# A gated mix of attention and GLU: earlier loads for the token mixtures, dense products thinned out over fourteen periods, and one early sigmoid in pieces

## The chip, the core and the metric

The program runs on one core of a Trainium2 chip. The metric is the device time of one execution in microseconds (us). The engines in the text are TensorE (PE in the profile, its weight loads PEld), VectorE (DVE), ScalarE (ACT), GpSimd (POOL) and SyncE (SP, which here issues all DMAs).

## What is computed

With x of 2048 tokens and 512 features:

```python
def _A_ref(x, wqkv, wo):                      # 32 heads of 16
    q, k, v = ...                             # x @ wqkv, by heads
    p = softmax(q @ k.T * Dh ** -0.5)
    return (p @ v) @ wo
def _B_ref(x, w_gate, w_up, w_down):          # F = 1792
    return (sigmoid(x @ w_gate) * (x @ w_up)) @ w_down
g = sigmoid((x * gate_w).sum(-1))
out = g * _A_ref(x) + (1 - g) * _B_ref(x)
```

All is float32 in and out. A dense product is made from three faster products of split operands: each operand is a high part (`h`, a rounded copy) and a low part (`l`, what the copy left over), and high x high, high x low and low x high are summed in PSUM.

## The kernel before, in words

**The main loop** (line 733 on) has 256 periods, `k`. A period belongs to one pair of heads and handles two key tiles. Its parts are generators, and a string of words says in which order TensorE calls them: `m0` and `m1` (line 695) make a score tile for head 0 or 1 of the pair 20 steps ahead and have VectorE take its row maximum (line 268); `t0` and `t1` (`st_part`, line 547) make scores the other way round with the maximum already taken off, and ScalarE writes their exponential (line 560); `d1` and `d0` (`dense`) put one matmul of the running dense product (`Sum.half`, line 150) on the upper or lower half of the array, so that it runs beside a score matmul on the other half. `values(k)` (line 666) closes the period with 16 matmuls of probabilities by values (line 674) into bank `seven[0]`, which the profile calls sm0. The digits in the words name PSUM banks: 0 to 3 are sm0 to sm3, 4 to 6 are st0 to st2, 7 is dn. The running dense product sums in dn.

The order is STEADY (eight m, eight t, six d1, six d0) for the first 239 periods, BARE (the same m and t, no dense product, dn used as an eighth score bank) for seven, and LAST (eight t, three d1, three d0; the maxima are all taken) for the last ten. From there on VectorE, not ScalarE, copies finished products and value sums out of PSUM.

**Tokens.** Both halves of the array write into dn. Between the upper and the lower half of a product stands a token: an empty GpSimd instruction (`turn`, line 161) that waits for the last upper matmul and on which the first lower one waits. GpSimd works in order, so a token also waits for what stands ahead of it there.

**Queues.** GpSimd's steps wait in lists: `later` (value sums, weight splits, the last maxima's row), `slow` (token mixtures, taken when `later` is empty) and `soon` (sums of finished products, moved to `later` at the period's end). `work(length)` puts out steps from these lists until their listed costs use up the length: after each turn and at the end of each period. `flush` puts out a whole list.

**Dense products.** A job list (`filling`, line 342) runs beside the attention: the remaining query and key columns, then the gate and up products by a scheme with fewer multiplications: `far`, `side` and `chain` products. `side` and `chain` need differences of token tiles, the mixtures, which `mix_x` (line 303) loads (line 308) and hands to GpSimd as differences and splits; four of them go out after the first four `far` jobs. Mixtures, key and query splits, old results (`had`) and late weights share two buffers, tag "ev"; product results and mixture halves share four, tag "er".

**The end** (line 824 on) takes 28 chunks (`n`) of 24 matmuls: hidden = sigmoid(gate) x up from memory (`hidden`, line 628), split in high and low (`hidden_split`, line 643), times the down weights (line 850), and between them eight groups of 24 matmuls for the attention's output (`heads_out`). Hidden values are loaded four chunks ahead. For chunks 0 and 1 `hidden_early` (line 634) makes the sigmoid inside the last periods from an exponential, since ScalarE's table holds the exponential there: 1/(1 + exp(-x)) with one VectorE reciprocal of 128x1024 each. `denominators` (line 647) loads the sums of the softmax, inverts them and stores them for `heads_load`: for one half of the heads in period 251, for the other at chunk 9.

Of the kernel before, what the change touches and what calls it, by code (L numbers as in the profile page):

```python
# [24 lines left out]
P = 128  # L25
# [13 lines left out]
FULL = 239  # L39
# [6 lines left out]
def gated_mix(ctx, tc, x, xT, wqk, wv, wo, w_gate, w_up, w_down, gate_w, out):  # L46
# [255 lines left out]

    def mix_x(c, k):


        one, two = [keep.tile([P, 2, 512], F32, name=f"mix{i}_{c}{k}", tag="ev", bufs=2) for i in range(2)]
        for to, (ci, ki) in ((one[:, 0], (c + 2, k)), (one[:, 1], (c, k)), (two[:, 0], (c + 2, k + 2)), (two[:, 1], (c, k + 2))):
            sp.dma_start(to, xT[ci, ki])

        def minus(to, u, w):  # L310
            slow.append((1.3, lambda: pool.tensor_tensor(to, u, w, ALU.subtract)))
        minus(one[:, 1], one[:, 0], one[:, 1])
        cols = slice((c + 2) * 512, (c + 3) * 512)
        split_later(xh[:, k, cols], xl[:, k, cols], one[:, 1], queue=slow)
        minus(one[:, 0], two[:, 0], one[:, 0])
        minus(two[:, 0], two[:, 0], one[:, 1])
        minus(two[:, 1], two[:, 1], two[:, 0])
        for n, t in enumerate((two[:, 0], one[:, 0], two[:, 1])):
            put_mix(n, c, k, t)
# [21 lines left out]
    def filling():  # L341
# [132 lines left out]
        for job, nxt in zip(jobs, jobs[1:]):  # L474
            due = len(later)
            kind, n = job
            coming = None
            for at, run in enumerate(sums_of(kind, n, ws)):
                if at == ask[kind][0]:
                    coming = raws(*nxt)  # L480
                if at == ask[kind][1]:
                    new = weights(*nxt, coming)
                    end = later[-1]
                yield run
            while end in later:
                later.pop(0)[1]()
            ws = new
            if kind == "far" and n < 4:
                flush(slow)
                mix_x(n // 2, n % 2)  # L490
            if kind == "far" and n == HF - 1:
                flush(slow)
                for c in range(2):
                    mixed_x(0, c, 2, c)
# [98 lines left out]
    eight = seven + [dn]  # L593
# [40 lines left out]
    def hidden_early(m):  # L634

        gu = loaded[m]
        act.activation(gu[:, 0], gu[:, 0], AF.Exp, scale=-1.0)
        dve.tensor_scalar(gu[:, 0], gu[:, 0], 1.0, 3e38, op0=ALU.add, op1=ALU.min)
        dve.reciprocal(gu[:, 0], gu[:, 0])  # L639
        dve.tensor_tensor(gu[:, 1], gu[:, 0], gu[:, 1], ALU.mult)  # L640

# [5 lines left out]
    def denominators(i):  # L647
        rows = slice(64 * i, 64 * i + 64)
        sp.dma_start(den[rows, :], pv_d[i].rearrange("p (c r) q -> (p c) r q", r=32)[:, DH, :])
        dve.reciprocal(den[rows, :], den[rows, :])  # L650
# [60 lines left out]
    def emit(order, **parts):  # L711

        for word in order.split():
            if word == "turn":
                turn(run)
                work(1.3)
            else:
                kind, _, b = word.partition(":")
                spot[:] = [eight[int(b)]] if b else []
# [5 lines left out]
    BARE = ("m1:7 t0:5 m1:2 t0:1 m1:3 t0:6 m1:0 t0:4 "  # L725
            "m0:7 t1:5 m0:2 t1:1 m0:0 t1:6 m0:3 t1:4")
# [6 lines left out]
    for k in range(NPER):  # L733
# [13 lines left out]
        emit(STEADY if k < FULL else BARE if k < FREE else LAST, **parts)  # L747
# [15 lines left out]
        if n == NSTEP - 10:  # L763
            denominators(0)
        if k == NPER - 2:
            raws = [late_raw(*late[m][:2]) for m in range(2)]
        if k in (NPER - 6, NPER - 4):
            hidden_early((k - NPER + 6) // 2)

    flush(later)  # L770
    bank = turns(banks)
    hidden_split(0, dve)
    act.activation(g1, logit, AF.Sigmoid)
    dve.tensor_scalar(g0, g1, -1.0, 1.0, op0=ALU.mult, op1=ALU.add)
# [3 lines left out]
    hidden(2)  # L778
# [33 lines left out]
    bankt = turns(maxb + [dn])  # L812
    bankh = turns(banks)
# [26 lines left out]
    for n, (c, f) in enumerate(chunks):  # L840
# [5 lines left out]
        for t in range(4):  # L846
# [4 lines left out]
            if (n, t) == (0, 1):  # L851
                values(NPER - 1)
                flush(later)
                hidden_split(1, dve)
# [4 lines left out]
        if n == 9:  # L859
            denominators(1)  # L860
# [36 lines left out]
```

## Time and profile before

| what | value |
|---|---|
| median of three runs | 1784.79 us (1781.0 to 1790.31) |
| the profiled execution | 1784.94 us |
| its span, first to last instruction | 1783.2 us, so 1.7 us lie around it |
| granted TensorE clock, mean | 0.977 |
| busy: PE, DVE, ACT, POOL | 1721.3, 1434.0, 1357.2, 873.2 us |

Rows of a group or of the timeline have start and length in us, engine, line, operation, "out<-in" with buffer numbers left out, shapes, a count, and in brackets the idle time just before and what ended it. Matmul ends are modelled and overlap. In windows each engine's entry is busy time and number of instructions; then come the granted clock, the share of the DMA engines and GB/s.

### The profile page before, as it was taken

What the parts mean: (1) busy time and instruction counts of PE and PEld (TensorE: products, weight loads), DVE (VectorE), ACT (ScalarE), POOL (GpSimd) and SP (SyncE); (2) the same over time, 40 slices, a digit from 0 to 9 for tenths busy, and PEclk for the clock granted to TensorE, in tenths of its full rate; (3) what the DMA queues carried; (4) which work ended last, traced back from release to release, by engine and by line L of the source; (5) the groups of instructions that cost most, each with busy time, mean ns of one, the idle gap of its engine ahead of it and who ended that gap; (6) DMA issues with size and microseconds to landing.
All of it is one profiled execution on the core that took longest, in us unless ns stands there. A gap on an engine that the chain in (4) does not pass through costs nothing.

```text
span 1783.2 us, 34285 instructions
## 1 busy us (share of the span) xinstructions
PE 1721.3 (97%) x12450; PEld 1040.4 (58%) x12450; DVE 1434.0 (80%) x2295; ACT 1357.2 (76%) x2631; POOL 873.2 (49%) x849
## 2 busy tenths in 40 slices
PE   9999999998899999999999999999999988698999
PEld 7755555554455555555555555555555543276787
DVE  6988888876789999998888888888888884653654
ACT  4288888877788888888888888888888886642321
POOL 1043434347635555555566666666666652352110
PEclk9999999999899999999999999999999997899999
DMA  9312414154645353536353535353434330186762
GB/s 250 76 50 58 94 58 94 58 123 169 181 132 143 98 123 106 110 107 159 134 125 112 125 114 125 114 126 115 124 115 126 115 126 8 52 259 217 234 200 76
DMA packets 124617, 219.83 MB, mean 123 GB/s; under 512 B 23008, under 2 KB 32992, under 8 KB 121568
## 3 DMA queue, kind: packets, MB, share of 16 engines
q1 hardware_dynamic: 124448, 217.64, 42.7%
q8 instruction: 98, 1.61, 0.4%
q14 instruction: 71, 0.58, 0.1%
HBM read 129.24 MB, written 88.34 MB: 122 GB/s over the span
## 4 chain that ended last, share of the span: by engine, by line
PE 88%; DVE 3%; DMA 3%; ACT 1%; issue 1%; POOL 1%; SPq 1%; POOLq 0%; DVEq 0%; ACTq 0%
PE dn L150 27%; PE sm L674 26%; PE sm L266 12%; PE st L558 6%; PE sm L850 4%; PE sm L558 4%; PE st L266 2%; PE st L137 2%; DVE stat L268 2%; PE st L150 1%; PE dn L850 1%; DMA gul<-gu_d 1%; PE st L524 1%; ACT p L560 1%; DVE gul L639 1%
## 5 line engine op out<-in xcount | busy, mean ns | idle before, releaser
L268 DVE TENSOR_REDUCE stat<-sm 128x1 f32<-128x512 f32 x1317 | 850.4, 681 | 176.4 <-PE sm L558 137.6
L560 ACT ACTIVATE p<-st 128x512 f32<-128x512 f32 x1034 | 620.7, 645 | 4.0 <-PE st L558 3.7
L560 ACT ACTIVATE p<-sm 128x512 f32<-128x512 f32 x1012 | 598.9, 627 | 31.3 <-PE st L558 17.4
L266 PE MATMUL sm<-ks,qs 48*128 48x512 f32 x1317 | 524.8, 439 | 5.3 <-DVE stat L268 4.8
L674 PE MATMUL sm<-p,v 128*17 128x512 f32 x4032 | 494.2, 608 | 6.8 <-DVE stat L268 6.8
L268 DVE TENSOR_REDUCE stat<-st 128x1 f32<-128x512 f32 x717 | 467.7, 680 | 0.2 <-PE st L266 0.2
L558 PE MATMUL st<-qs,ks 64*128 64x512 f32 x1034 | 436.3, 425 | 0.0
L558 PE MATMUL sm<-qs,ks 64*128 64x512 f32 x1012 | 426.7, 424 | 0.6 <-ACT p L560 0.6
L266 PEld LDWEIGHTS sm<-ks,qs 48*128 48x128 f32 x1317 | 240.5, 185 | 298.9 <-DVE stat L268 215.9
L691 POOL TENSOR_TENSOR sum<-sum,part 128x512 f32<-128x512 f32 x224 | 289.1, 1291 | 246.9 <-PE sm L558 213.0
L266 PE MATMUL st<-ks,qs 48*128 48x512 f32 x717 | 283.1, 395 | 0.0
L679 ACT ACTIVATE part<-sm 128x512 f32<-128x512 f32 x215 | 128.9, 599 | 153.1 <-issue 114.2
L674 PEld LDWEIGHTS sm<-p,v 128*17 128x17 f32 x4032 | 94.5, 98 | 242.6 <-issue 163.4
L558 PEld LDWEIGHTS st<-qs,ks 64*128 64x128 f32 x1034 | 192.4, 187 | 30.9 <-issue 5.7
L558 PEld LDWEIGHTS sm<-qs,ks 64*128 64x128 f32 x1012 | 188.2, 187 | 11.4 <-issue 4.3
L466 POOL TENSOR_TENSOR had<-chain,had 128x512 f32<-128x512 f32 x84 | 108.0, 1285 | 64.3 <-PE sm L558 36.1
L266 PEld LDWEIGHTS st<-ks,qs 48*128 48x128 f32 x717 | 133.8, 187 | 1.4 <-ACT v L541 0.3
L466 POOL TENSOR_TENSOR chain<-chain,chain 128x512 f32<-128x512 f32 x84 | 108.6, 1293 | 23.0 <-PE st L558 11.7
L100 POOL TENSOR_TENSOR ol<-ot,oh 128x1024 fp32r<-128x1024 f32 x8 | 19.3, 2413 | 122.3 <-ACT oh L97 110.8
L466 POOL TENSOR_TENSOR side<-side,side 128x512 f32<-128x512 f32 x28 | 36.2, 1291 | 79.6 <-PE sm L558 74.2
L497 ACT ACTIVATE chain<-dn 128x512 f32<-128x512 f32 x107 | 73.7, 689 | 0.0
L850 PE MATMUL sm<-wd_h,hl 128*128 128x512 f32 x208 | 67.4, 391 | 0.0
(752 smaller groups left out, 3149.0 us busy)
## 6 DMA issues: line engine op xcount, KB each, us to landing
gul<-gu_d SPq DMA_DIRECT2D x56, 512.0 KB
had<-gu_d SPq DMA_DIRECT2D x84, 256.0 KB
gu_d<-had SPq DMA_DIRECT2D x84, 256.0 KB
gu_d<-side SPq DMA_DIRECT2D x56, 256.0 KB
qs<-q_d SPq DMA_DIRECT2D x90, 128.0 KB
ks<-k_d SPq DMA_DIRECT2D x90, 128.0 KB
pv_d<-sum SPq DMA_DIRECT2D x32, 256.0 KB
gu_d<-far SPq DMA_DIRECT2D x28, 256.0 KB
```

What stands on the lines that cost most here:

```text
L137: pe.matmul(o, a, b, start=(i == 0), stop=(i == len(ops) - 1))
L150: mm = pe.matmul(self.o, a[rows], b[rows], start=(self.n == 0), stop=(self.n == 2 * len(self.ops) - 1))
L266: pe.matmul(t, qs[r:r + KM, qt * P:(qt + 1) * P], ks[r:r + KM, g * 512:(g + 1) * 512], start=True, stop=True)
L268: dve.tensor_reduce(stat[half][:, b, qt % 8, g:g + 1], t, axis=AX.X, op=ALU.max)
L466: pool.tensor_tensor(to, u, w, ALU.add)
L497: leave = lambda e, o: act.activation(e, o, AF.Copy)
L558: pe.matmul(o, ks[r:r + KR, (kt + a) * P:(kt + a + 1) * P], qs[r:r + KR, q0:q0 + 512], start=True, stop=True)
L560: act.activation(pt[:, 2 * a + c, :], o, AF.Exp, scale=DH ** -0.5)
L674: pe.matmul(o[32 * c:32 * c + VW, :], v[:, 2 * k % 16 + a, h * VW:(h + 1) * VW], pts[c // 2][:, 2 * a + c % 2, :], start=(a == 0), stop=(a ...
L679: act.activation(e, o, AF.Copy)
L691: pool.tensor_tensor(s, s, e, ALU.add)
L850: pe.matmul(down[t], a, b, start=(f == 0 and m == 0), stop=(f == NF - 2 and m == 5))
```

## The change

Five edits are made together.

1. `mix_load` is split from `mix_x`: the loads of mixture u go out at product 6u + 2 of the `far` jobs, its GpSimd steps at product 6u + 4. Before, both stood after job u.
2. After each turn `work` is given 2.0, not 1.3.
3. STEADY ends at period 232; periods 232 to 245 use HALF, which is STEADY with three d1 and three d0 left out and the same banks; BARE is gone.
4. Only chunk 0 has its sigmoid from the exponential. It begins in period 249, the reciprocal is four pieces of 128x256, one a period, and the split into hl0 follows in period 254. Chunk 1 takes ScalarE's sigmoid after the loop and its split on ScalarE; chunk 2's sigmoid comes after chunk 0's matmuls.
5. `denominators` becomes a generator of load, two reciprocals of 64x256, and store: the first half loads in period 250 and is inverted at chunks 0 and 1, the second loads at chunk 1, is inverted at chunks 5 and 6, and is stored at chunk 7. The banks of the end's products are dealt out anew.

```diff
-FULL = 239
+FULL = 232
...
+    def mix_load(c, k):
+        tiles = mixing[c, k] = [keep.tile([P, 2, 512], F32, name=f"mix{i}_{c}{k}", tag="ev", bufs=2) for i in range(2)]
+        for t, ki in zip(tiles, (k, k + 2)):
+            for a, ci in enumerate((c + 2, c)):
+                sp.dma_start(t[:, a], xT[ci, ki])
...
+                if kind == "far":
+                    u, r = divmod(4 * n + at - 2, 6)
+                    if r == 0 and u < 4:
+                        flush(slow)
+                        mix_load(u // 2, u % 2)
+                    if r == 2 and u < 4:
+                        mix_x(u // 2, u % 2)
...
-            if kind == "far" and n < 4:
-                flush(slow)
-                mix_x(n // 2, n % 2)
...
-        dve.reciprocal(gu[:, 0], gu[:, 0])
+        yield
+        for a in range(2):
+            for cols in (slice(0, 256), slice(256, 512)):
+                dve.reciprocal(gu[:, 0, a, cols], gu[:, 0, a, cols])
+                yield
         dve.tensor_tensor(gu[:, 1], gu[:, 0], gu[:, 1], ALU.mult)
+        hidden_split(m, dve)
+        yield
...
-        dve.reciprocal(den[rows, :], den[rows, :])
+        yield
+        for cols in (slice(0, 256), slice(256, 512)):
+            dve.reciprocal(den[rows, cols], den[rows, cols])
+            yield
...
-                work(1.3)
+                work(2.0)
...
-    BARE = ("m1:7 t0:5 m1:2 t0:1 m1:3 t0:6 m1:0 t0:4 "
-            "m0:7 t1:5 m0:2 t1:1 m0:0 t1:6 m0:3 t1:4")
+    HALF = ("m1:3 t0:2 m0:4 d1 t0:5 m0:6 d1 t0:1 m0:3 d1 t0:2 turn m0:0 t1:4 "
+            "m1:5 d0 t1:1 t1:6 d0 m1:2 m1:3 t1:4 d0")
...
-        if n == NSTEP - 10:
-            denominators(0)
+        if k == NPER - 6:
+            dens = [denominators(i) for i in range(2)]
+            next(dens[0])
...
-        if k in (NPER - 6, NPER - 4):
-            hidden_early((k - NPER + 6) // 2)
+        if k == NPER - 7:
+            early = hidden_early(0)
+        if k >= NPER - 7:
+            next(early, None)
 
     flush(later)
-    bank = turns(banks)
-    hidden_split(0, dve)
+    bank = turns(banks[:1])
     act.activation(g1, logit, AF.Sigmoid)
+    hidden(1)
...
-    hidden(2)
...
-    bankt = turns(maxb + [dn])
-    bankh = turns(banks)
+    bankt = turns([maxb[1], banks[2], maxb[2], maxb[3], dn])
+    bankh = turns([maxb[0], banks[0], banks[1]])
...
-        if n == 9:
-            denominators(1)
+        if n == 0:
+            hidden(2)
+        if n < 3:
+            next(dens[0], None)
+        if n in (1, 5, 6, 7):
+            next(dens[1], None)
```

SyncE's queue around the first mixture, before: stores of the four first `far` products (gu_d is their place in memory), then the four loads of the mixture's two tiles mix0 and mix1.

```order
L428 DMA gu_d_75<-far00_0_4094 128x512
L428 DMA gu_d_75<-far00_1_4162 128x512
L428 DMA gu_d_75<-far10_0_4223 128x512
L428 DMA gu_d_75<-far10_1_4284 128x512
L308 DMA mix0_00_4287<-in_xT_dram 128x512 x2
L308 DMA mix1_00_4288<-in_xT_dram 128x512 x2
```

After:

```order
L434 DMA gu_d_75<-far00_0_4094 128x512
L434 DMA gu_d_75<-far00_1_4162 128x512
L309 DMA mix0_00_4165<-in_xT_dram 128x512 x2
L309 DMA mix1_00_4166<-in_xT_dram 128x512 x2
L434 DMA gu_d_75<-far10_0_4229 128x512
L434 DMA gu_d_75<-far10_1_4290 128x512
```

The loads moved two products ahead, from behind the stores of far10 to ahead of them.

TensorE in a BARE period, from its seventh score matmul (the fourth for a maximum) to its last, before (line 266 is a score for a maximum, line 558 one for an exponential):

```order
L266 MATMUL sm_69<-ks_102,qs_101 128x512
L558 MATMUL st_65<-qs_99,ks_100 128x512
L266 MATMUL dn<-ks_102,qs_101 128x512
L558 MATMUL st_66<-qs_101,ks_102 128x512
L266 MATMUL sm_71<-ks_102,qs_101 128x512
L558 MATMUL sm_70<-qs_101,ks_102 128x512
L266 MATMUL sm_69<-ks_102,qs_101 128x512
L558 MATMUL st_67<-qs_101,ks_102 128x512
L266 MATMUL sm_72<-ks_102,qs_101 128x512
L558 MATMUL st_65<-qs_101,ks_102 128x512
```

The second part of a HALF period, from the last score matmul ahead of its turn to the period's end (line 567 is the old 558; line 150 is the dense product in dn):

```order
L567 MATMUL sm_71<-qs_101,ks_102 128x512
L266 MATMUL sm_69<-ks_102,qs_101 128x512
L567 MATMUL st_65<-qs_101,ks_102 128x512
L266 MATMUL st_66<-ks_102,qs_101 128x512
L150 MATMUL dn<-xh,ca(1, 6)h 128x512
L567 MATMUL sm_70<-qs_101,ks_102 128x512
L567 MATMUL st_67<-qs_101,ks_102 128x512
L150 MATMUL dn<-xl,ca(1, 6)h 128x512
L266 MATMUL sm_71<-ks_102,qs_101 128x512
L266 MATMUL sm_72<-ks_102,qs_101 128x512
L567 MATMUL st_65<-qs_101,ks_102 128x512
L150 MATMUL dn<-xh,ca(1, 6)l 128x512
```

Bank dn is no longer a score bank, six dense matmuls stand in each period, and sm0 (sm_69) is written once by a score instead of twice.

VectorE in the LAST periods, before (gul are the hidden values of chunks 0 and 1, part are copies of value sums, chain copies of finished products):

```order
L681 COPY part249_17561<-st1_66 128x512
L681 COPY part250_17600<-st2_67 128x512
L638 TENSOR_SCALAR gul0_0_17519<-gul0_0_17519 128x1024
L639 RECIPROCAL gul0_0_17519<-gul0_0_17519 128x1024
L640 TENSOR_TENSOR gul0_0_17519<-gul0_0_17519 128x1024
L409 COPY chain16_11_17632<-dn_68 128x512
L681 COPY part251_17644<-sm3_72 128x512
L650 RECIPROCAL den_94<-den_94 64x512
L681 COPY part252_17687<-sm0_69 128x512
L638 TENSOR_SCALAR gul0_2_17522<-gul0_2_17522 128x1024
L639 RECIPROCAL gul0_2_17522<-gul0_2_17522 128x1024
L640 TENSOR_TENSOR gul0_2_17522<-gul0_2_17522 128x1024
```

After:

```order
L698 COPY part249_17575<-st1_66 128x512
L646 TENSOR_SCALAR gul0_0_17533<-gul0_0_17533 128x1024
L698 COPY part250_17616<-st2_67 128x512
L650 RECIPROCAL gul0_0_17533<-gul0_0_17533 128x256
L415 COPY chain16_11_17646<-dn_68 128x512
L698 COPY part251_17658<-sm3_72 128x512
L650 RECIPROCAL gul0_0_17533<-gul0_0_17533 128x256
L698 COPY part252_17699<-sm0_69 128x512
L650 RECIPROCAL gul0_0_17533<-gul0_0_17533 128x256
L415 COPY chain16_12_17728<-dn_68 128x512
L698 COPY part253_17738<-sm1_70 128x512
L650 RECIPROCAL gul0_0_17533<-gul0_0_17533 128x256
```

The two reciprocals of 128x1024 and the denominators' are out of these rows; four of 128x256 stand one by one between the copies.

More of the change, by code (lines that the diff above doesn't have):

```diff
@@ L301, in quarter @@
         return [((w[0][:, k, :], w[1][:, k, :]), (xh[:, k0 + k, cols], xl[:, k0 + k, cols])) for k in range(2)]
+    mixing = {}
+    def mix_load(c, k):
[3 more added lines that the diff above has]
+                sp.dma_start(t[:, a], xT[ci, ki])
     def mix_x(c, k):
-        one, two = [keep.tile([P, 2, 512], F32, name=f"mix{i}_{c}{k}", tag="ev", bufs=2) for i in range(2)]
-        for to, (ci, ki) in ((one[:, 0], (c + 2, k)), (one[:, 1], (c, k)), (two[:, 0], (c + 2, k + 2)), (two[:, 1], (c, k + 2))):
-            sp.dma_start(to, xT[ci, ki])
+        one, two = mixing.pop((c, k))
         def minus(to, u, w):
@@ L474, in filling @@
         for job, nxt in zip(jobs, jobs[1:]):
-            due = len(later)
             kind, n = job
@@ L592, in gated_mix @@
     seven = maxb + banks
-    eight = seven + [dn]
     bank7 = turns([seven[b] for b in (5, 1, 6, 2, 3, 4, 0)])
@@ L715, in emit @@
                 turn(run)
-                work(1.3)
+                work(2.0)
             else:
                 kind, _, b = word.partition(":")
-                spot[:] = [eight[int(b)]] if b else []
+                spot[:] = [seven[int(b)]] if b else []
                 next(parts[kind], None)
@@ L746, in gated_mix @@
         parts["t0"], parts["t1"] = st_part(k, 0), st_part(k + 1, 1) if k + 1 < NPER else iter(())
-        emit(STEADY if k < FULL else BARE if k < FREE else LAST, **parts)
+        emit(STEADY if k < FULL else HALF if k < FREE else LAST, **parts)
         if run and run.done():
@@ L853, in gated_mix @@
                 flush(later)
-                hidden_split(1, dve)
+                hidden_split(1)
             if f == NF - 2:
```

## The prediction

> **What bounds the kernel now.** I read the page first, then the stages by windows, then waits, chain and timeline where a stage is longer than its own rate.
>
> ```profile
> span 1783.2 us, 34285 instructions
> PE 1721.3 (97%) x12450; PEld 1040.4 (58%) x12450; DVE 1434.0 (80%) x2295; ACT 1357.2 (76%) x2631; POOL 873.2 (49%) x849
> PE 88%; DVE 3%; DMA 3%; ACT 1%; issue 1%; POOL 1%; SPq 1%; POOLq 0%; DVEq 0%; ACTq 0%
> ```
>
> TensorE holds the chain nearly everywhere, so only stretches in which it waits or runs at a lower clock can shrink. The windows of line 674 alone (columns: length, PE busy with count, weight loads, granted clock, DMA) count periods, since every period has 16 such matmuls:
>
> ```profile
> 478.70:1446.33 967.63, 330.70 (x2768) 64.04 (x2768) 1.00 0.43 121
> 369.90:484.28 114.38, 34.71 (x256) 6.28 (x256) 0.90 0.49 154
> 1446.33:1498.94 52.61, 18.46 (x112) 2.97 (x112) 0.84 0.23 71
> 1498.94:1553.51 54.57, 20.75 (x144) 4.02 (x144) 0.81 0.11 35
> ```
>
> The long stretch is 2768/16 = 173 STEADY periods of 967.63/173 = 5.593 us. The mixture stage has 16 periods in 114.38, where 16 x 5.593 = 89.5 would do: 24.9 lost. The seven BARE periods take 52.61, 7.52 each, although they have the least TensorE work. Nine LAST periods take 54.57, 6.06 each. The whole windows say what LAST could be, and how long the end is (columns: PE, PEld, DVE, ACT, POOL):
>
> ```profile
> 1504.43:1519.97 15.54, 15.54 (x121) 6.83 (x120) 4.15 (x6) 15.54 (x33) 5.00 (x5) 1.00 0.14 45
> 1553.51:1783.20 229.69, 209.98 (x908) 166.99 (x906) 114.47 (x101) 72.47 (x79) 51.67 (x23) 0.95 0.60 195
> ```
>
> Four undisturbed LAST periods take 15.54/4 = 3.885, with ScalarE busy throughout.
>
> **Part 1, the mixtures.**
>
> ```profile
> 377.38 1.87 SPq L308 DMA_DIRECT2D mix<-in_xT_dram  x4
> ```
> ```profile
> 381.78 1.26 POOL L311 TENSOR_TENSOR mix<-mix 128x512 f32<-128x512 f32 x1 [6.53 <-DMA mix<-in_xT_dram]
> ```
> ```profile
> POOL mix L311 <- DMA mix<-in_xT_dram: 18.4, 4, 6.5
> PEld dn L150 <- POOLq L161: 17.1, 5, 6.4
> ```
> ```profile
> 386.75 3.29 PE sm L674 x16
> ...
> 1424.06 1.85 PE sm L674 x16
> ```
>
> GpSimd stands at the first difference until the load lands, and the token on which TensorE's other half waits (line 161) is queued behind it: 18.4 us of one wait are 17.1 us of the other. The rest of the 24.9 is the half clock after each stop (the chain shows 3.29 us for the 16 value matmuls at 386.75 where 1.85 is usual) and GpSimd steps flushed at once. The loads go out two periods, 11.2 us, earlier; one took from 377.38 to 381.78, 4.4 us. They now stand on SyncE ahead of two products' stores and of later weights, and wait there for the two "ev" tiles; GpSimd frees those one to two periods before. So 24.9 goes, and what is late next is GpSimd's own work. Of a mixture that is eight wide steps and four copies:
>
> ```profile
> 383.11 0.61 POOL L127 CAST xh<-mix 128x512 fp32r<-128x512 f32 x1
> 383.80 1.27 POOL L124 TENSOR_TENSOR xl<-mix,xh 128x512 fp32r<-128x512 f32 x1
> ```
>
> 8 x 1.27 + 4 x 0.61 = 12.6 us, over four periods beside the sums and the weights. By the order of GpSimd's instructions the fullest stretches between two tokens hold three wide steps and two 256-wide splits (0.40 and 0.73 each, rows in part 2): 3 x 1.27 + 2 x 1.13 = 6.07, 0.5 more than a period, twice; six more lie between 5 and 5.8. I take 2 left. It can be 0; it can be 8, if each of the eight waits 1 us more for a buffer whose store is under way. **-22.9**.
>
> **Part 2, work(2.0).** In every STEADY turn GpSimd now takes a second step right after the token. The work is the same; it is bunched.
>
> ```profile
> 560.87 1.29 POOL L466 TENSOR_TENSOR side<-side,side 128x512 f32<-128x512 f32 x1 [4.31 <-DMA qs<-q_d]
> 563.36 0.73 POOL L388 TENSOR_TENSOR side_8r<-side_8r 128x256 f32<-128x256 f32 x1
> 567.98 0.40 POOL L127 CAST side(0, 1)h<-side_1r 128x256 fp32r<-128x256 f32 x1
> ```
> ```profile
> 478.70:1446.33 967.63, 967.63 (x7614) 559.00 (x7612) 862.69 (x1461) 866.69 (x1731) 592.79 (x589) 1.00 0.43 121
> ```
>
> On average GpSimd works 592.79/173 = 3.43 of 5.59. But once in each of 12 side products a stretch now holds two wide sums, four 256-wide steps and a copy: 2 x 1.29 + 4 x 0.73 + 0.40 = 5.90, 0.31 too long; once in each of 13 chain products about 3 x 1.29 + 2 x 0.61 + 0.73 = 5.82, 0.23 too long. If all of it reaches TensorE it costs 12 x 0.31 + 13 x 0.23 = 6.7. It can't gain, since nothing gets shorter. It costs nothing if the token behind a stretch is posted when the last step starts and not when it ends, since each excess is shorter than one step; no row here shows which. The stretches after it are short, so nothing adds up, and I take a value near the low end: **+1**.
>
> **Part 3, HALF for BARE.** Seven STEADY and seven BARE periods become fourteen HALF periods; no product is added or dropped. What sets a period is seen on VectorE and at the value matmuls:
>
> ```profile
> 1426.37 0.69 DVE L268 TENSOR_REDUCE stat<-sm 128x1 f32<-128x512 f32 x1 [0.71 <-PE sm L558]
> 1426.98 1.28 DVE L268 TENSOR_REDUCE stat<-st 128x1 f32<-128x512 f32 x2
> 1428.18 1.28 DVE L268 TENSOR_REDUCE stat<-sm 128x1 f32<-128x512 f32 x2
> ...
> 1429.97 1.27 DVE L268 TENSOR_REDUCE stat<-sm 128x1 f32<-128x512 f32 x2
> ```
> ```profile
> 1429.57 0.13 PEld L674 LDWEIGHTS sm<-p,v 128*17 128x17 f32 x8 [0.26 <-DVE stat L268]
> ```
>
> The values are summed in bank sm0, which the fifth maximum of the period reads last: values (1.85), the first score matmul after them (0.43 in the chain below), five maxima from 1426.37 to 1429.46, a tenth, values again: 5.5. In BARE the bank's second use is the seventh maximum, and the chain of waits shows the loop:
>
> ```profile
> 1453.10 1.91 PE sm L674 x16
> 1455.01 0.43 PE dn L266
> 1455.49 4.28 DVE stat L268 x7
> 1459.81 1.91 PE sm L674 x16
> ```
>
> 1459.81 - 1453.10 = 6.71 with the same reductions. HALF has STEADY's bank order with six of twelve products taken out, so its loop is STEADY's, 5.59, and TensorE has room. 7 x 5.593 + 52.61 = 91.8 becomes 14 x 5.593 = 78.3: **-13.5**. Below that: the eight maxima alone run from 1426.37 to 1431.24, 4.87, or 68 for fourteen periods. Above: the clock.
>
> ```profile
> 1473.16:1498.94 25.78, 20.79 (x96) 6.68 (x96) 14.61 (x26) 14.09 (x28) 2.57 (x2) 0.70 0.00 1
> ```
>
> In three BARE periods it fell to 0.70 and they took 8.59 each; fourteen such would be 120. How much TensorE works tells the cases apart, as an estimate: two matmuls side by side on the array's halves at 0.227 (5.44 for 24 in the chain, quoted in part 5), and the values at 1.85. HALF is 11 x 0.227 + 1.85 = 4.35 of 5.59, 78%; BARE 8 x 0.227 + 1.85 = 3.67 of 6.71, 55%; LAST, which kept 1.00 over the four periods above, 7 x 0.227 + 1.85 = 3.44 of 3.885, 89%. HALF is nearer to LAST; I take full clock.
> The Trainium skill, "TensorE: Matmul & The Clock Gate", section "A second HAM failure mode: psum-queue depth-cycling", says that a kernel cycling through PSUM banks leaves micro-gaps often enough to swing between half and full clock; HALF has such gaps in every period. By that rule the 13.5 would not come and the sum would give 1734; it is a rival below. The trace agrees for BARE (0.70) and not for STEADY, which cycles the same banks (1.00 over 967.63 us).
>
> **Part 4, the early sigmoid.**
>
> ```profile
> 1522.90 0.95 ACT gul L637
> ...
> 1525.06 6.56 DVE gul L639
> ...
> 1541.77 6.56 DVE gul L639
> ...
> 1558.83 2.19 DVE hl L100
> 1561.07 4.63 PE sm L850 x10
> ```
>
> Two reciprocals of 6.56 us hold VectorE, on which the copies out of PSUM now wait in line: two periods of over 11 us, and the half clock behind them. One goes (chunk 1 gets ScalarE's sigmoid after the last exponential), the other is four pieces of 6.56/4 = 1.64, each in one period between two copies of 0.69; VectorE then works about 2.7 to 3.4 of 3.885. The first denominators' reciprocal leaves this stage too. So nine periods of 3.885 = 35.0, plus ScalarE's early exponential 0.95, plus 0.7, an estimate without a row, for the last maxima: they go through GpSimd and two DMAs into the query tile, and with no half clock ahead of them LAST wants them sooner. 36.6 for 54.57 is **-18.0**. If half of each piece is felt it is 3.3 less; at LAST's rate alone it is -19.6.
>
> **Part 5, the end.** The denominators of the second half are loaded and inverted four chunks before they are needed.
>
> ```profile
> DVE den L650 <- DMA den<-pv_d: 15.1, 1, 15.1
> ```
> ```profile
> 1642.35:1660.00 17.65, 8.08 (x30) 6.24 (x29) 12.00 (x9) 4.66 (x5) 2.42 (x1) 0.71 0.65 205
> 1608.20:1620.00 11.80, 8.95 (x32) 0.86 0.70 257
> ```
> ```profile
> 1671.92 5.44 PE sm L850 x24
> ```
>
> 30 matmuls at the chunk's rate (the chain has 5.44 for 24) are 6.8 of 17.65: 10.9 lost to that one wait and the half clock. It goes; the loads of the chunks behind it, which were queued beside it, are late next: I allow 2. At the start, hl0 no longer stands behind the last product's copy (2.19 at 1558.83), and chunk 0 can start at full clock (4.63 for 10 matmuls was half). But around 1610 data comes at 257 GB/s and TensorE waits for it: 11.80 for 32 matmuls, 32 x 0.227 = 7.3, is 4.5 lost, and what is won before that point is mostly waited out there; I count 2 of it. Together **-11**, bounds -5 and -16. The PSUM banks dealt out anew, g1 and the sigmoid of chunk 2 a step later cost nothing while ScalarE is 72.47/229.69 busy here.
>
> Sum: -22.9 + 1 - 13.5 - 18.0 - 11 = -64.4. The profiled execution took 1784.94 (span 1783.2 and 1.7 around it), 0.15 above the median shown: 1784.94 - 64.4 = 1720.5.
>
> **The rivals.** *Clock in HALF*: half clock in half or all of the periods; 7 to 14 of 8.59 for 5.59 add 21 to 42: 1742 to 1762. For it: BARE, and the skill's rule; against it: 79% of work. 0.09. *Late tokens*: the long stretches of part 2 and of the mixtures reach TensorE in full, 6.7 + 8: 1732. 0.10. *The loads are not early*: SyncE comes to them late because it stands at a store or an "ev" tile; 18 of the 22.9 stay: 1739. 0.07. *The end refills*: data, not the denominators, bound it; part 5 gives 2: 1730. 0.09. *Slower*: the second step of each turn waits for a ScalarE copy or a load still under way, so that the token is late in every one of the 168 side and chain periods, not in 25. At 0.5 us each that is 84: 1804. It decides from 64.4/168 = 0.38 us a period, and from 0.44 it is beyond half a per cent. Against it: 3.43 of 5.59 on average. 0.03.
>
> **How the numbers follow.** About 0.5% (8.9 us) can be told from no change. Forecast 0.62, its own range 1712 to 1731; the rivals 0.38. Up to 1746 take in late tokens, refill, late loads and the mild clock case. Below, the shorter HALF and the bounds of parts 1 and 5 give 1708. Faster 0.95, same 0.02, slower 0.03.
>
> **What would show it.** Periods of line 691 at 5.59 through the mixtures, with no GpSimd wait for mix; HALF at 5.6 and clock 1.00; no LAST period over 5; no wait of VectorE for den, and TensorE unbroken from 1620's counterpart on. A HALF clock under 0.9, tokens waited for in the side products, or a new wait above 5 us in the end would prove it wrong.

## The result, and the profile after

The changed kernel takes 1724.85 us (median of 4 runs, 1723.71 to 1726.0) beside 1782.89 us of the kernel before (4 runs): a ratio of 0.9667, 95% interval 0.9637 to 0.9698. The forecast was 1720.5 in 1708 to 1746. The profiled execution has a span of 1721.9 us where the one before had 1783.2.

The page after, for the whole program: span, busy time by engine, and the shares of the chain that ended last.

```profile
span 1721.9 us, 34323 instructions
PE 1704.4 (99%) x12450; PEld 1040.2 (60%) x12450; DVE 1433.3 (83%) x2297; ACT 1357.0 (79%) x2632; POOL 874.9 (51%) x849
PE 93%; DMA 2%; POOL 1%; ACT 1%; DVE 1%; issue 1%; SPq 0%; POOLq 0%; ACTq 0%; DVEq 0%
```

The work is the same (PE x12450, POOL 874.9 for 873.2); what went is time in which TensorE waited or ran at half clock.

The windows of the value matmuls alone (line 691, the old 674), after, cut between the same value matmuls as before: the mixture stage of 16 periods, the steady stretch, fourteen HALF periods, nine LAST periods.

```profile
369.70:463.50 93.80, 30.58 (x256) 5.90 (x256) 0.99 0.54 163
463.50:1386.90 923.40, 315.94 (x2640) 61.05 (x2640) 1.00 0.45 124
1386.90:1464.95 78.05, 26.76 (x224) 5.19 (x224) 1.00 0.28 90
1464.95:1501.95 37.00, 17.55 (x144) 3.77 (x144) 1.00 0.24 75
```

The mixture stage lost 20.6 (it was 114.38) and still holds 93.80 - 89.5 = 4.3 more than sixteen steady periods. HALF is 78.05/14 = 5.575 a period at a granted clock of 1.00. The nine LAST periods are 4.11 each. The steady stretch is 2640/16 = 165 periods of 5.596; before, the same 165 took 922.9.

The waits of the mixture stage, after (us in total, times, longest):

```profile
POOL mh L330 <- DMA gu_d<-far: 3.7, 1, 3.7
PEld dn L150 <- POOLq L161: 3.3, 2, 2.6
```

No step of a mixture waits for its load any more. What GpSimd still waits for are buffers whose stores are under way: 3.7 us in period 66 (9.18 us long), and 1.9 for the store of a mixture half in period 55 (6.38 long).

VectorE in one LAST period, after: a copy out of PSUM, a piece of the reciprocal, the next copy.

```profile
1488.46 0.69 DVE L698 COPY part<-st 128x512 f32<-128x512 f32 x1 [1.84 <-PE st L691]
1489.07 1.74 DVE L650 RECIPROCAL gul<-gul 128x256 f32<-128x256 f32 x1
1490.73 0.63 DVE L415 COPY chain<-dn 128x512 f32<-128x512 f32 x1
```

The piece takes 1.74 and the copy behind it comes at once. The whole of the end, then the same matmuls on, and the same 17.65 us long, as the stretch in which VectorE waited for the denominators before:

```profile
1502.01:1721.90 219.89, 207.76 (x907) 165.79 (x906) 127.68 (x106) 76.27 (x84) 53.19 (x24) 0.98 0.62 204
1592.00:1609.65 17.65, 17.65 (x79) 14.61 (x79) 12.52 (x11) 5.99 (x7) 2.41 (x1) 1.00 0.69 232
```

Where 17.65 us held 30 matmuls at clock 0.71 they now hold 79 without a gap. The end is 219.89, 9.7 less by the same cut. What TensorE still waits for there stands at its start (timeline of TensorE, after):

```profile
1507.98 0.47 PE L869 MATMUL sm<-wd0h,hl 128*128 128x512 f32 x1 [1.99 <-DVE hl L99]
1509.15 0.79 PE L869 MATMUL sm<-wd0h,hl 128*128 128x512 f32 x1 [0.46 <-DVE hl L100]
1538.43 0.50 PE L869 MATMUL sm<-wd_l,hl 128*128 128x512 f32 x1 [1.58 <-POOL wd_l L100]
```

Stage by stage, against the terms of the prediction:

| stage | predicted | measured |
|---|---|---|
| mixtures | -22.9 | -20.6 |
| steady stretch, work(2.0) | +1 | +0.5 |
| HALF for STEADY and BARE | -13.5 | -13.7 |
| LAST | -18.0 | -17.6 |
| end | -11 | -9.7 |
| up to the mixtures | 0 | -0.2 |
| sum | -64.4 | -61.3 |

So each term is right to within 2.3 us. Whether their reasons are is another question; the experiments took each apart.

### The profile page after: what moved, and what is told of

The parts are those of the page before. It is cut to its first block, busy times and chain, and to the rows that moved or that the text cites. A ratio compares the mean times of both kernels' runs of the same rounds, so it can differ in the third digit from the quotient of the medians.

```text
span 1721.9 us, 34323 instructions
## 1 busy us (share of the span) xinstructions
PE 1704.4 (99%) x12450; PEld 1040.2 (60%) x12450; DVE 1433.3 (83%) x2297; ACT 1357.0 (79%) x2632; POOL 874.9 (51%) x849
## 4 chain that ended last, share of the span: by engine, by line
PE 93%; DMA 2%; POOL 1%; ACT 1%; DVE 1%; issue 1%; SPq 0%; POOLq 0%; ACTq 0%; DVEq 0%
PE dn L150 28%; PE sm L691 27%; PE sm L266 12%; PE st L567 6%; PE sm L567 5%; PE sm L869 4%; PE st L266 3%; PE st L137 2%; PE st L150 2%; PE dn L869 2%; DMA gul<-gu_d 1%; PE st L533 1%; PE st L869 1%; PE sm L137 1%; ACT p L569 1%
## 5 line engine op out<-in xcount | busy, mean ns | idle before, releaser
L569 ACT ACTIVATE p<-sm 128x512 f32<-128x512 f32 x1026 | 606.7, 627 | 4.0 <-PE st L567 3.1
L691 PE MATMUL sm<-p,v 128*17 128x512 f32 x4032 | 482.6, 596 | 0.0
L268 DVE TENSOR_REDUCE stat<-st 128x1 f32<-128x512 f32 x738 | 481.4, 680 | 0.2 <-PE st L266 0.2
L567 PE MATMUL st<-qs,ks 64*128 64x512 f32 x1020 | 427.1, 419 | 0.0
L266 PE MATMUL st<-ks,qs 48*128 48x512 f32 x738 | 291.5, 395 | 0.0
L567 PEld LDWEIGHTS st<-qs,ks 64*128 64x128 f32 x1020 | 187.8, 184 | 30.3 <-issue 3.4
L266 PEld LDWEIGHTS st<-ks,qs 48*128 48x128 f32 x738 | 137.7, 187 | 1.7 <-ACT v L550 0.3
L640 DVE TENSOR_TENSOR gul<-gul 128x1024 f32<-128x1024 f32 x27 | 40.0, 1482 | 28.8 <-DMA gul<-gu_d 16.6
```

The source lines that it names most:

```text
L266: pe.matmul(t, qs[r:r + KM, qt * P:(qt + 1) * P], ks[r:r + KM, g * 512:(g + 1) * 512], start=True, stop=True)
L268: dve.tensor_reduce(stat[half][:, b, qt % 8, g:g + 1], t, axis=AX.X, op=ALU.max)
L567: pe.matmul(o, ks[r:r + KR, (kt + a) * P:(kt + a + 1) * P], qs[r:r + KR, q0:q0 + 512], start=True, stop=True)
L569: act.activation(pt[:, 2 * a + c, :], o, AF.Exp, scale=DH ** -0.5)
L691: pe.matmul(o[32 * c:32 * c + VW, :], v[:, 2 * k % 16 + a, h * VW:(h + 1) * VW], pts[c // 2][:, 2 * a + c % 2, :], start=(a == 0), stop=(a ...
```

## Experiments

All times are medians beside runs of the kernel before on the same chip. Where a run's edit sits in one stage, that stage is read from its trace. The runs of one kernel lie 1 to 6 us apart, and the kernel before was run at 1775.5 to 1790.3. Where a stage's code is the same, the traces agree to 0.2 us in the HALF periods, but less well elsewhere: the mixture stage took 92.6 to 95.0 in the six traces that share the code of the kernel after there. Unless said otherwise a run starts from the kernel after.

### The mixtures: loads, spacing, work

The edit of the change has three parts: loads ahead of the steps, six products (periods) between mixtures instead of four, and work(2.0). **loads_with_steps** undoes the first:

```diff
                     if r == 0 and u < 4:
                         flush(slow)
-                        mix_load(u // 2, u % 2)
                     if r == 2 and u < 4:
+                        mix_load(u // 2, u % 2)
                         mix_x(u // 2, u % 2)
```

> The kernel after, with the loads of a mixture put out at product 6u + 4, right ahead of its GpSimd steps, and no longer two products sooner; the steps stay where the change put them. Theory (the lead of the loads is what the change won): GpSimd stands at each of four first differences for about 4.5 us again, tokens behind it, so the sixteen periods from the 50th on take about 110 us, not 93.8, and the whole about 1740 (15 to 20 more than 1724.85). Rival (the place of the steps in the program did it, the loads' lead is spare): the sixteen periods stay within 3 us of 93.8 and the time within 1722 to 1729.

1731.89 us, and 100.15 for the sixteen periods: between the two. Only the first of four mixtures waited (6.6 us, one wait of GpSimd for mix); the loads of the other three stood right ahead of their steps and were in time all the same. The prediction's reason for this term did not hold, so a new theory was needed, and **mix_four_apart** undid the spacing as well (loads and steps after every fourth product):

> The kernel after, with loads and steps of a mixture after every fourth product again (a period each, so 22.3 us apart), as before; work(2.0) stays. Since the loads right ahead of their steps, but six products apart, cost only one stall (100.2 for the sixteen periods from value matmul 50 on, not 114.4), the theory now is the spacing: one mixture's steps took 22.4 us on GpSimd, so at four products the next loads wait for the last steps that were flushed, and GpSimd waits behind them each time: 108 to 115 for the sixteen periods, 1738 to 1746. Rival (work(2.0) empties the queue in time, so spacing does not matter): one stall as with six, 100 to 102, 1730 to 1733.

1734.19 us, 103.80 for the sixteen periods, three waits for mix of 13.0 together: again between the two. **work_1_3** undid work alone:

```diff
-                work(2.0)
+                work(1.3)
```

> The kernel after, with work(1.3) after each turn as before; mixtures six products apart and loaded early as after. First theory (the prediction's: work(2.0) only bunches GpSimd's steps): the steady stretch from value matmuls 66 to 231, 923.4 in after, within 1 us, and the mixture stage (value matmuls 50 to 66, 93.8 in after) within 2 us: 1722 to 1727. Second theory (work(2.0) draws the mixture's steps in time, so that fewer are left for the flush): mixture stage 4 to 10 us longer, 1729 to 1735.

1725.45 us, 94.80 and 922.9: the first theory holds: taken as a whole, work(2.0) is worth about nothing beside the two others. Its one stall, period 63, is not GpSimd's:

```profile
PE st L567 <- DMA qs<-max_d: 3.5, 1, 3.5
```
```profile
435.26 2.04 SPq L309 DMA_DIRECT2D mix<-in_xT_dram  x4
437.40 0.38 SPq L286 DMA_DIRECT2D max_d<-mhl  x1
...
442.04 2.79 SPq L290 DMA_DIRECT2D qs<-max_d  x4
```

The row of the maxima (max_d) went out on SyncE right behind four early mixture loads, could be read back only from 442.04 on, and TensorE waited for it. **six_apart_alone** has both undone, so that only the spacing is left of the change:

> The kernel after, with the loads right ahead of the steps (product 6u + 4) and work(1.3), so that of the change's edits for the mixtures only the spacing of six products is left. The sixteen periods from value matmul 50 on were 114.4 before, 103.8 with work(2.0) alone, 100.2 with work(2.0) and spacing, 93.8 with all three, 94.8 with spacing and early loads. Theory (work and spacing are two ways to the same end, the first mixture done before the second is loaded): 99 to 102 for the sixteen periods, 1730 to 1733 for the whole. Rival (they add up): 107 to 111, 1738 to 1743.

1726.74 us and 96.05: less than either theory gave. One wait for mix is left, 6.4 us at the first mixture. The windows of the value matmuls for the four runs (each its own sixteen periods; in order loads_with_steps, mix_four_apart, work_1_3, six_apart_alone):

```profile
369.90:470.05 100.15, 31.37 (x256) 5.97 (x256) 0.96 0.52 154
```
```profile
369.85:473.65 103.80, 32.42 (x256) 6.14 (x256) 0.97 0.52 171
```
```profile
370.20:465.00 94.80, 30.64 (x256) 5.91 (x256) 0.98 0.52 158
```
```profile
369.75:465.80 96.05, 31.68 (x256) 6.02 (x256) 0.96 0.49 146
```

Set out by edit, for the sixteen periods:

| | work(1.3) | work(2.0) |
|---|---|---|
| four apart, loads with steps | 114.4 (before) | 103.8 |
| six apart, loads with steps | 96.1 | 100.2 |
| six apart, loads early | 94.8 | 93.8 (after) |

The spacing alone is worth 18.3 of the 20.6. Early loads add 1.3 or 6.4 to it, work(2.0) takes 10.6 off without the spacing; with it, it gains 1.0 or costs 4.1. The small differences are sums of larger ones. By the periods of these traces, early loads remove the stall at the first mixture (11.04 and 6.68 us for periods 52 and 53 in six_apart_alone, 5.59 and 5.58 in work_1_3) and, with work(1.3), bring the one at period 63 (10.80).

And work(2.0) is not free here. In all seven traces with the spacing, work(2.0), the old place of the pair's loads and a steady period of 5.58, period 66 takes 8.0 to 10.4 us; in the three with work(1.3) it takes 5.58. The copy of a mixture half that waits there, in the kernel after and then in six_apart_alone:

```profile
460.26 0.61 POOL L330 CAST mh<-mix 128x512 fp32r<-128x512 f32 x1 [3.75 <-DMA gu_d<-far]
```
```profile
467.46 0.61 POOL L330 CAST mh<-mix 128x512 fp32r<-128x512 f32 x1 [1.95 <-DMA gu_d<-far]
```

With work(2.0) GpSimd comes to this copy sooner after the store has gone out and stands at it for 3.75, with a token behind it; with work(1.3) it comes later and no period is longer for it. Period 55 goes the same way: 6.4 in those seven traces, 5.58 in the three. So the 4.3 that the kernel after still holds come with work(2.0).

Why the spacing decides: GpSimd and SyncE at the second mixture, before:

```profile
406.58 1.28 POOL L330 TENSOR_TENSOR ml<-mix,mh 128x512 fp32r<-128x512 f32 x1
413.44 1.26 POOL L311 TENSOR_TENSOR mix<-mix 128x512 f32<-128x512 f32 x1 [5.58 <-DMA mix<-in_xT_dram]
```
```profile
408.40 2.67 SPq L308 DMA_DIRECT2D mix<-in_xT_dram  x4
```

and in six_apart_alone:

```profile
406.03 1.28 POOL L336 TENSOR_TENSOR ml<-mix,mh 128x512 fp32r<-128x512 f32 x1
414.90 1.28 POOL L317 TENSOR_TENSOR mix<-mix 128x512 f32<-128x512 f32 x1 [2.89 <-PE sm L567]
```
```profile
410.11 1.86 SPq L309 DMA_DIRECT2D mix<-in_xT_dram  x4
```

In the kernel before, one mixture's steps run on GpSimd from 381.78 to 407.9, 26 us, while four products are 22.3. There the second mixture came due while the first was still under way: its last steps were flushed, its loads could go out only when the last of them had given the tiles free, and GpSimd stood at the next difference, with the tokens behind it, until they landed. With 33.5 us between mixtures the loads go out at nearly the same moment (410.11 for 408.40), but GpSimd's next difference is not yet due: it waits 2.89 us for TensorE, not for the load. SyncE runs ahead of the other engines here as far as its own waits let it, so a load needs no lead in the program where SyncE has nothing else to wait for.

**pair_load_later** asks for the stall of period 66 that is left in the kernel after:

```diff
-        if n % 32 == 0 and n // 32 + 1 < NPAIR:
+        if n % 32 == 4 and n // 32 + 1 < NPAIR:
             load_pair(n // 32 + 1)
```

> The kernel after, with the loads of the next pair of heads put out two periods later in each 16 (period 2, not 0). In after, period 66 takes 9.18 us since the store of a far product waits on SyncE and in the DMA queues behind these twelve loads, and GpSimd's copy of a mixture half waits for that store's buffer. Theory (the collision at period 64 is the 3.6 us, and the 0.5 behind it): period 66 at 5.6 to 6, 3 to 4 us less, 1720 to 1722. Rival (GpSimd's flushed steps alone are too long there): no change in period 66, 1724 to 1726.

1724.39 us. Period 66 is at its 5.58, so the twelve loads of the next pair were what delayed the store. But periods 69 and 70 took 9.85 and 7.06, because the weights of the last far product now came late behind the same loads:

```profile
POOL far06h L127 <- DMA far06r<-in_w_gate_dram: 5.7, 1, 5.7
```

The collision moved and the time stayed.

### HALF: bank order, not thinning

**bare_in_half_order** keeps STEADY to period 238 and then leaves out all dense products for seven periods, as before, but in HALF's bank order:

```diff
-FULL = 232
+FULL = 239
...
+    BARE = ("m1:3 t0:2 m0:4 t0:5 m0:6 t0:1 m0:3 t0:2 m0:0 t1:4 "
+            "m1:5 t1:1 t1:6 m1:2 m1:3 t1:4")
...
-        emit(STEADY if k < FULL else HALF if k < FREE else LAST, **parts)
+        emit(STEADY if k < FULL else BARE if k < FREE else LAST, **parts)
```

> The kernel after, with STEADY to period 238 and then seven periods without any dense product, as before, but with the bank order of HALF (sm0 read by the fifth maximum and not by the seventh). Work of TensorE as an estimate: 8 x 0.227 + 1.85 = 3.67 of 5.58, 66%. Theory (the second use of sm0 made the period 6.71 long, and the half clock came because TensorE then stood idle 45% of the time): periods of 5.58; whether 66% keeps the clock is open, if it does the time is that of after, 1724 to 1727. Rival (any stretch without dense products loses the clock, whatever the bank order): clock under 0.85 in the last three or four of them and periods over 7, 8 to 20 more: 1733 to 1745.

1723.27 us. The seven periods (value matmuls alone) take 39.01, 5.573 each, at full clock:

```profile
1425.36:1464.37 39.01, 13.38 (x112) 2.59 (x112) 1.00 0.29 96
```

So the 13.7 us come from HALF's order of scores and banks alone; spreading the spare products over fourteen periods adds nothing that can be measured. And an estimated 66% of TensorE's time in use keeps the clock for 39 us, where BARE's 55% had lost it after 27. Whether the share decides, or how the idle time lies within a period, was not tried.

**sum_bank_fourth** (on the version end_reordered, below) tests the loop itself: if the fifth maximum, which reads sm0 last, sets the period, let the fourth read it.

```diff
-    STEADY = ("m1:3 t0:2 m0:4 d1 d1 t0:5 m0:6 d1 d1 t0:1 d1 m0:3 d1 t0:2 turn m0:0 t1:4 "
+    STEADY = ("m1:3 t0:2 m0:4 d1 d1 t0:5 m0:6 d1 d1 t0:1 d1 m0:0 d1 t0:2 turn m0:3 t1:4 "
...
-    HALF = ("m1:3 t0:2 m0:4 d1 t0:5 m0:6 d1 t0:1 m0:3 d1 t0:2 turn m0:0 t1:4 "
+    HALF = ("m1:3 t0:2 m0:4 d1 t0:5 m0:6 d1 t0:1 m0:0 d1 t0:2 turn m0:3 t1:4 "
```

> As end_reordered, and in STEADY and HALF the banks of the fourth and the fifth maximum of a period are exchanged, so that sm0, into which the values are summed, is read last by the fourth maximum and not by the fifth. Theory of the prediction (values, first score, the maxima up to sm0's, values again set the period of 5.58): the period falls by up to one reduction of 0.64, held by TensorE's own work of 14 x 0.227 + 1.85 = 5.03 and VectorE's 4.99: 5.1 to 5.4, and 240 periods save 45 to 115 us: 1605 to 1675. Rival (TensorE's matmuls between the values, which stand nearly without a gap, set it as much): periods 5.5 to 5.6, 1700 to 1724. If ScalarE's copy out of sm0 comes too late for the fourth maximum, periods are longer than 5.6 and the time is over 1730.

1855.66 us: slower, and not for the reason named for that case. Every period is 6.18. VectorE's reductions and TensorE's matmuls in one of them:

```profile
763.17 1.28 DVE L268 TENSOR_REDUCE stat<-sm 128x1 f32<-128x512 f32 x2
```
```profile
764.50 0.50 PE L266 MATMUL sm<-ks,qs 48*128 48x512 f32 x1 [0.36 <-DVE stat L268]
765.16 1.91 PE L691 MATMUL sm<-p,v 128*17 128x512 f32 x16
```

The two reductions are the fourth and the fifth maximum; the fifth ends at 764.45. It now reads sm3, and sm3 is also the bank of the eighth score, which stands ahead of the values in TensorE's order. So that score waits for the fifth maximum, and the values start 0.66 behind it: the same loop, with a piece of TensorE's work more in it. The period grew by 0.60. In both orders the wait that ends last is for the fifth maximum, so the loop through it is shown; that a shorter one exists in seven banks is not.

### The early sigmoid and the end

**one_reciprocal** puts the four pieces back into one instruction:

```diff
-        for a in range(2):
-            for cols in (slice(0, 256), slice(256, 512)):
-                dve.reciprocal(gu[:, 0, a, cols], gu[:, 0, a, cols])
-                yield
+        yield
+        dve.reciprocal(gu[:, 0], gu[:, 0])
+        yield
+        yield
+        yield
```

> The kernel after, with the one early sigmoid's reciprocal as one instruction of 128x1024 in period 251 in place of four pieces of 128x256 in 250 to 253; nothing else moves. Theory (an instruction of 6.56 us holds the copies out of PSUM, TensorE stops and comes back at half clock): one period of 9 to 11 us where 3.93 stood, and 5 to 8 us more: 1730 to 1733. Rival (the number of reciprocals and their place cost, not the length of a piece; the other banks cover one such wait): under 2 us more.

1730.66 us, 5.8 more. VectorE, and TensorE behind it:

```profile
1495.25 6.54 DVE L649 RECIPROCAL gul<-gul 128x1024 f32<-128x1024 f32 x1
1501.71 0.63 DVE L699 COPY part<-sm 128x512 f32<-128x512 f32 x1
```
```profile
1502.39 0.79 PE L567 MATMUL sm<-qs,ks 64*128 64x512 f32 x1 [2.45 <-DVE part L699]
```

The copy waits out the reciprocal, TensorE waits 2.45 for the copy and comes back at half clock (0.79 for this matmul; a like one takes 0.49 at 1503.93 in the kernel after). The nine periods take 42.5 for 37.0. The loss is spread over two periods (7.12 and 6.21), not in one of 9 to 11; the size fits the first theory. The profiled run was the slowest of the four, 1735.28 us: its end took 3.8 more than in the kernel after as well, for which no edit of this run accounts.

**denominators_late** puts the second half's denominators back to chunk 9:

```diff
-        if n in (1, 5, 6, 7):
-            next(dens[1], None)
+        if n == 9:
+            for _ in dens[1]:
+                pass
```

> The kernel after, with the second half's denominators loaded, inverted and stored at chunk 9 as before, in two pieces of 64x256. Theory (the wait of VectorE for their load in front of the chunks' multiplications is the whole gain in the end): TensorE stops once for 8 to 10 us and loses 1 to 2 more at half clock: 9 to 11 more, 1734 to 1736, in one place near the fourteenth chunk. Rival (the end is bound by the chunks' own loads, and any gain there is waited out again): under 4 more.

1736.11 us, 11.3 more. In the trace the end is 12.3 longer, and 10.8 of it stand in one place, chunk 11; VectorE in the end:

```profile
DVE den L666 <- DMA den<-pv_d: 14.1, 1, 14.1
```

The end was not bound by other data there; this wait was nearly the whole loss.

**early_sooner** and **end_reordered** try what the kernel after still waits for at the start of the end. The first loads chunk 0's hidden values and begins its sigmoid a period sooner:

```diff
-        if n == NSTEP - 16:
+        if n == NSTEP - 18:
...
-        if k == NPER - 7:
+        if k == NPER - 8:
             early = hidden_early(0)
-        if k >= NPER - 7:
+        if k >= NPER - 8:
```

> The kernel after, with the hidden values of chunk 0 loaded and the early sigmoid begun one period sooner, so that hl0 is split in period 253's place and not in 254's. Theory (TensorE waits at the first chunk 1.99 and 0.46 us for VectorE's split, and runs the next matmuls at half clock): the interval of the 255th value matmuls, 11.23 in after, at 6.6 to 8, 3 to 4.5 less in that place; of it a part may be waited out at chunk 2 where weights and data come late (4.3 us in after): 1720 to 1724 for the whole. Rival (all of it is waited out at chunk 2): interval shorter, time 1724 to 1726.

1724.92 us. The interval fell from 11.23 to 7.23 as expected, the end from its first instant only from 219.9 to 217.7; the rest was waited out, and in the median nothing shows. end_reordered adds another order for ScalarE:

```diff
+        late_next()
+        if n + 2 < len(chunks):
+            hidden_split(n + 2)
         if n + 3 < len(chunks):
             hidden(n + 3)
-        if n + 2 < len(chunks):
-            hidden_split(n + 2)
...
-        late_next()
```

> A version that may be better: the kernel after with the early sigmoid a period sooner, and in each chunk of the end the late weights' split and the split of the hidden values two chunks ahead issued in front of the sigmoid three chunks ahead, which waits for its load (ScalarE waited 39.3 us for such loads in the end, with the splits behind it). Theory (ScalarE's order, not the data, makes TensorE wait between 1523 and 1540): the end from the 254th value matmuls on, 219.9 in after and 217.8 with the early sigmoid sooner, at 212 to 215; 1718 to 1721. Rival (the loads bound it, whatever the order): 217 to 218, as with the early sigmoid alone, 1722 to 1725.

1717.84 us, 7.0 less than after; the end is 211.7. ScalarE's wait for the hidden values' loads, after and then in end_reordered:

```profile
ACT gul L639 <- DMA gul<-gu_d: 39.3, 10, 9.6
```
```profile
ACT gul L639 <- DMA gul<-gu_d: 2.8, 1, 2.8
```

The splits that TensorE needs next no longer stand behind a sigmoid that waits for a load. The first hidden values of the end are loaded no sooner, but from chunk 5 on the loads go out sooner as well (chunk 7's at 1532.24, not at 1538.87): on SyncE they stand behind the load of late weights, which goes out when a split has set its buffer free (in the kernel after at 1538.40, GpSimd's split ending at 1538.37).

### A better version

**first_lead_only** joins what the runs showed: end_reordered, HALF's order without products for seven periods, work(1.3), and an early load for the first mixture alone.

```diff
                     if r == 0 and u < 4:
                         flush(slow)
+                    if u < 4 and r == (2 if u else 0):
                         mix_load(u // 2, u % 2)
```

> The version that the runs point to: end_reordered with work(1.3), the early load for the first mixture alone (the three others are loaded right ahead of their steps, six products apart), and STEADY to period 238 followed by seven periods without dense products in HALF's bank order. Theory (with six products between mixtures only the first one's loads are late, because SyncE stands at four stores of far products ahead of them): the sixteen periods from value matmul 50 on at 89.5 to 91 (96.1 with no early load, one stall of 6.6 in it; 93.8 in after), and the whole 1711 to 1715. Rival (a stall of 3 to 5 us comes back somewhere else, as when the loads of the next pair were moved): 93 to 96 for the sixteen, 1716 to 1719.

1709.66 us (5 runs, 1708.53 to 1712.16), a ratio to the kernel before of 0.9595, 95% interval 0.9568 to 0.9622: 15 us better than the change (13 by the two ratios; the runs were on different chips). Its span, its sixteen periods of the mixtures and its end:

```profile
span 1706.8 us, 34287 instructions
```
```profile
369.70:459.15 89.45, 30.58 (x256) 5.90 (x256) 1.00 0.52 156
```
```profile
1496.17:1706.70 210.53, 203.68 (x907) 163.68 (x906) 124.77 (x105) 76.72 (x84) 52.04 (x24) 1.00 0.65 213
```

The mixtures cost nothing any more: 89.45 is sixteen steady periods. With six products between mixtures only the first one's loads are late enough to cost time, because SyncE comes to them behind four stores that wait for products (366.05 to 377.33 in the trace before). The second mixture's still make GpSimd wait 2.1 us here, and no period is longer for it. With work(1.3) the stall of period 66 is gone as well, and without early loads for the later mixtures that of period 63.

## Why the prediction was right, and where its reasons were not

**Mixtures.** The term was right (-22.9 for -20.6) for the wrong reason. The step that failed: "The loads go out two periods, 11.2 us, earlier", put forward as what removes the waits. It holds for the first mixture alone; that the size came out was luck as far as this reason goes. The change gives the places 6u + 2 and 6u + 4; the working looked at the 2 between load and steps and not at the 6 between mixtures, which had been 4. It does say that GpSimd frees the two "ev" tiles in time, but not that the six products are what makes it so. The trace before held the clue: a mixture's 12.6 us of steps "over four periods" beside the rest of GpSimd's work ran from 381.78 to 407.9, longer than the four products to the next one. What is late next was named rightly (a buffer whose store is under way, 0 to 8); it was 4.3, not 2. It needs both the pair's loads, which the prediction did not have, and work(2.0), which its sum priced only in the steady stretch.

**work(2.0).** In the steady stretch nothing reached TensorE: 923.4 beside 922.9 before, and the difference is the 0.5 of one period behind the mixtures' stall. The excess stretches of 0.31 and 0.23 us cost nothing, in line with a token that is posted when the last step starts, though no run shows that moment itself. The rival of a wait in every side and chain period is out. The rival of late tokens is out for the side and chain products; in the mixture stage work(2.0) did make tokens late, at periods 55 and 66.

**HALF.** The size (-13.5 for -13.7) and the loop are borne out twice, by the same order without products and by the exchange of two banks that lengthened it. The thinning, which the prediction used to argue for the clock, was not needed. On the clock, the rival by the Trainium skill ("TensorE: Matmul & The Clock Gate", section "A second HAM failure mode: psum-queue depth-cycling") did not happen here: HALF cycles seven banks for 78 us at 1.00, and so do seven periods with no dense product. BARE, at 0.70 in its last three periods, remains the only stretch looked at here that fits that section.

**LAST.** -17.6 for -18.0. one_reciprocal shows that the length of the instruction decides: four pieces of 1.74, 6.96 together, cost 5.8 less than one of 6.54. The 0.7 for the last maxima has no row behind it and none was found: in the trace after, no wait of these nine periods is for the row of the maxima. What lengthens the first two, 4.42 and 4.53 long where the next two take 3.84 and 3.83, are waits of 0.69 and 0.65 for a token.

**End.** -9.7 for -11. The wait for the denominators was mis-sized by little: counted from one chunk to the same chunk it gave 11.3, and denominators_late took 11.3 back. The step that failed is "I count 2 of it", the gain at the start. Up to the old wait the new kernel had lost 1.2. Chunk 2 still began 1.9 sooner than before, but TensorE then waited inside chunks 2 and 4 for splits, and chunk 5 began 4.3 later than before; some of that was made up by chunk 9. ScalarE's splits stood behind its wait for loads, as in this row, after which the late weights' low part, waited for at 1538.43 above, could be made:

```profile
1532.52 1.06 ACT L639 ACTIVATE gul<-gul 128x1024 f32<-128x1024 f32 x1 [7.02 <-DMA gul<-gu_d]
```

The rival *the end refills* named the data as the bound; end_reordered shows that it was the order of ScalarE's work in front of the data, which also held back the later loads.

Five right sums from five stages did not make five right reasons: undoing the parts one by one moved the largest term to another edit of the same change.

## What to carry to other kernels

Ask of periodic work not only when its loads go out but whether one round ends before the next begins: steps that last 26 us and are called for every 22 us hold up the next round's loads (early loads at that spacing were not tried). A queue that runs ahead and has nothing else to wait for needs no lead in the program, and an early load can harm what stands behind it in that queue. On an in-order engine put the instruction that may wait for data behind those that others wait for, and cut a long one into pieces that fit between the copies around it.

## What was not expected of the hardware

In the kernel after a store of 128x512 (256 KB) that SyncE issued behind the twelve loads of 128 KB for the next pair was under way for 6 us, as the chain of waits shows, while the four loads of a mixture, as large each, took 4.4 together before.

```profile
454.14 5.99 DMA gu_d<-far
```

In work_1_3 the row of the maxima, a store of 32 KB right behind four loads of 256 KB, took over 4 us (issued at 437.40, read back from 442.04), and TensorE felt 3.5 of it; in the kernel after, with no such loads right ahead, the same row took 2.6 (434.96 to 437.57). And the clock stayed at 1.00 for 39 us with TensorE idle, by the estimate, a third of each period.
